# Attention recast per pair of chunks, k gated from PSUM, MLP units of one PSUM bank, and a new instruction planner, in a one-core attention and mixer kernel

## The chip, the cores and the metric

The kernel runs on one core of one Trainium2 chip. The metric is device time in microseconds (us); lower is better. A run counts as fast or slow by its time against the fastest of the same kernel; comparisons here use fast runs, and where a trace fell on a slow run the text says so. "Before" is the unchanged kernel, "after" the changed one. Engines: PE is TensorE (matmul), PEld its weight loads, DVE is VectorE, ACT is ScalarE, POOL is GpSimd, SP is SyncE. SBUF is the on-chip memory that holds tiles and weights; PSUM is the one that the matmuls write, eight banks here, and an *eviction* is a copy out of it.

## The reference

A gated linear recurrence per head, then a token mixer and a channel mixer. Batch 4, 8 heads, sequence 768, head size 48, model size 384, token hidden 256, channel hidden 1536.

```python
f = 1.0 / (1.0 + np.exp(-f_logit))
for t in range(S):
    state = f[:, :, t, :, None] * state + einsum('bhd,bhe->bhde', k[:, :, t], v[:, :, t])
    y[:, :, t] = einsum('bhd,bhde->bhe', q[:, :, t], state)
x = y.transpose(0, 2, 1, 3).reshape(B, S, H * D)
h  = relu(x.T @ w_tok1) @ w_tok2          # over tokens
u  = x + h.T
out = u + relu(u @ w_ch1) @ w_ch2         # over channels
```

The sequence is cut into 6 chunks of 128 rows. The kernel loads two chunks at a time (a *pair*, d = 0 to 2), so there are 12 pairs in all. Within a pair each SBUF partition holds two neighbouring tokens (j = 0 and 1). q is scaled by a decay G, k by its inverse Gi, so that a masked product of the two gives the recurrence inside a chunk; a state of 48 by 48 per head carries it between chunks.

## The kernel before

A planner in Python simulates five engines, decides the order of instructions on each, and chooses buffers. The engines then work through those orders strictly, waiting on semaphores. PSUM is four tiles of two banks each, shared by everything:

```python
P.pool("PP", [pt([128, 2, 512], FP32, f"pp{i}") for i in range(4)])
```

v is needed in chunk order, so two casts put it in place and two more shift half of it over partitions, for each pair. Gi is a bf16 tile in SBUF, and both gates multiply two SBUF operands on VectorE:

```python
nc.gpsimd.tensor_copy(o[0:64, 0:2], x[0:64])        # v, POOL
nc.gpsimd.tensor_copy(o[64:128, 1:3], x[64:128])
cast(e, o[64:128, 0], x[0:64, 1])                   # v shifted, POOL (or ACT in batch 0)
cast(e, o[0:64, 2], x[64:128, 0])
...
nc.scalar.activation(P[f"Gi{i}"], sv(), AF.Exp, bias=0.0, scale=1.0)
...
for j in range(2):                                  # the gates, L408
    nc.vector.tensor_tensor(gated(z, nm, j), x[:, j], gg[:, j], ALU.mult)
```

The second token weight is loaded as it lies and reordered by two copies, which the planner gives to POOL:

```python
P.op("w2", {"DVE": (0.6, 0.1), "POOL": (1.6, 0.1)}, ["w2s0", "w2s1"], ["w2"], lambda e: [cast(
    e, w_tok2[:, kt].rearrange("r c (two p) -> r c p two", two=2),
    P[f"w2s{kt}"].rearrange("r (c p two) -> r c p two", p=64, two=2)) for kt in range(2)], 50)
```

The channel mixer works on whole two-bank tiles, both halves of the tokens together, and its ReLU eviction takes 768 columns. Priorities are fixed numbers per batch:

```python
p_tok, p_ch1, p_ch2 = 100 * b + 60, 100 * b + 165, 100 * b + 178
...
for kt in range(3):
    nc.tensor.matmul(pm[:, th, 0:384]..., lhsT=w_ch1[:, kt, cc * 128:(cc + 1) * 128],
                     rhs=uT[:, 3 * th:3 * th + 3, kt, :], start=(kt == 0), stop=(kt == 2))
```

Lines to know in the profile of before: L604 and L635 are the first and second channel matmuls, L537 and L557 the token matmuls, L408 the gates, L467 the masks, L305 a cast helper.

Of the kernel before, what the change touches and what calls it, by code (L numbers as in the profile page):

```python
# [29 lines left out]
class Op:  # L30
    __slots__ = ("name", "eng", "ins", "outs", "fn", "prio", "after", "done", "start", "groups", "xfer",
                 "pipe")


class Planner:


    def __init__(self):
        self.ops, self.by_name = [], {}
        self.pools, self.group_pool, self.group_of = {}, {}, {}  # L40
        self.producers, self.touch = {}, {}

    def pool(self, name, slots):
        self.pools[name] = [[s, 0.0] for s in slots]

# [5 lines left out]
    def op(self, name, eng, ins, outs, fn, prio, after=(), xfer=None):  # L51
        o = Op()
        o.name, o.eng, o.ins, o.outs, o.fn, o.prio = name, eng, tuple(ins), tuple(outs), fn, prio
        o.after, o.done, o.start, o.xfer = tuple(after), None, None, xfer
        assert name not in self.by_name, name
        self.by_name[name] = o
        self.ops.append(o)

    def run(self):
# [26 lines left out]
        slot_of, last = {}, {}  # L86
        order = []
        while ready:
            best = None
            for o in ready:  # L90
# [7 lines left out]
                for p, n in need.items():  # L98
                    f = sorted(s[1] for s in self.pools[p] if s[1] is not None)
                    if len(f) < n:  # L100
                        ok = False
                        break
                    t = max(t, f[n - 1])
                if not ok:
                    continue
                for e, (occ, lat) in o.eng.items():
                    st = max(t, free.get(e, 0.0))
                    key = (round(st, 3), o.prio, st + occ)
                    if best is None or key < best[0]:
                        best = (key, o, e, st)  # L110
# [3 lines left out]
            free[e] = st + occ  # L114
            end = st + occ + lat
# [10 lines left out]
            for g in o.groups:  # L126
                p = self.group_pool.get(g)
                if p is not None and g not in slot_of:
# [6 lines left out]
                if self.touch[g] == 0 and g in slot_of:  # L135
                    slot_of[g][1] = last[g] + SEM
# [10 lines left out]
        self.slots = {g: s[0] for g, s in slot_of.items()}  # L147
# [3 lines left out]
    def __getitem__(self, v):  # L151
        return self.slots[self.group_of[v]]
# [3 lines left out]
def kernel(  # L156
# [38 lines left out]
    msk = st([128, 128], BF16, "msk")  # L195
# [4 lines left out]
    w_tok2 = st([128, 2, NCH, 128], BF16, "w_tok2")  # L200
# [9 lines left out]
    P.pool("U", [st([128, 3, DM], BF16, f"v_bf{i}") for i in range(3)])  # L210
    P.pool("G", [st([128, 2, H, D], BF16, f"G{i}") for i in range(2)])
    P.pool("Gi", [st([128, 2, H, D], BF16, f"Gi{i}") for i in range(2)])
# [4 lines left out]
    P.pool("gl", [st([128, HP, 2], FP32, f"glast{i}") for i in range(3)])  # L217
    st_tiles = [st([128, HP, D], FP32, f"state{i}") for i in range(2)]
    P.pool("st", st_tiles)
    bd_tiles = [st([128, HP, D], BF16, f"state_bf{i}") for i in range(3)]  # L220
# [6 lines left out]
    P.pool("z", [st([128, S], BF16, f"zT{i}") for i in range(13)])  # L227
    P.pool("PP", [pt([128, 2, 512], FP32, f"pp{i}") for i in range(4)])


    def consts():
# [13 lines left out]
        nc.vector.tensor_copy(msk, tri)  # L245
        nc.vector.tensor_copy(msk[0:64, 64:128], tri[0:64, 0:64])
        nc.vector.tensor_copy(msk[64:128, 0:64], strict[64:128, 64:128])
        for t in st_tiles:
# [13 lines left out]
    for b in range(B):  # L262
        seq = [(nm, c + 1 if nm == "f" else c) for c in range(-1, NP) for nm in "fqkv"]
        prev = None
        for n, (nm, d) in enumerate([s for s in seq if 0 <= s[1] < NP]):
            load(nm, b, d, (100 * b - 150 if b else -1000) + n,
# [17 lines left out]
    for kt in range(2):  # L284
        P.value(f"w2s{kt}", f"w2s{kt}", "z")
    P.op("w2l", {"POOL": (1.2, 0)}, [], ["w2s0", "w2s1"], lambda: [nc.gpsimd.dma_start(
        out=P[f"w2s{kt}"], in_=moe_w_tok2[128 * kt:128 * kt + 128]) for kt in range(2)], -898, ["~w1"],
        xfer=w_mb["w2"] / 0.38)
    P.op("w2", {"DVE": (0.6, 0.1), "POOL": (1.6, 0.1)}, ["w2s0", "w2s1"], ["w2"], lambda e: [cast(
        e, w_tok2[:, kt].rearrange("r c (two p) -> r c p two", two=2),  # L290
        P[f"w2s{kt}"].rearrange("r (c p two) -> r c p two", p=64, two=2)) for kt in range(2)], 50)
    for nm, dst, src, pr, dep in (("wc1", w_ch1, moe_w_ch1, -897, "w2l"),
# [21 lines left out]
    def attention(b, d):  # L314
        i, pr = f"{b},{d}", 100 * b + 20 * d - 70
# [3 lines left out]
        for nm, pl in (("U", "U"), ("G", "G"), ("Gi", "Gi"), ("qkT", "qkT"), ("qkT", "qkT"), ("gl", "gl"), ("xb", "xb"), ("S", "PP"),  # L319
                       ("y", "PP"), ("dS", "PP"), ("x", "x"), ("Pf", "Pf"), ("L", "L")):  # L320
            P.value(f"{nm}{i}", f"{nm}{i}", pl)
        for e in range(2):
            P.value(f"qkT{i},{e}", f"qkT{i}", "qkT")
        P.value(f"qh{i}", f"qk{i}", "qk")
# [4 lines left out]
        P.value(f"S1{i}", f"S{i}", "PP")  # L329
# [3 lines left out]
        def kblk(r, j, hp):  # L333
            t = P[f"kh{i}"][r, H * 128:]
            n = (2 * hp + j) if xbar else (4 * j + hp)
            return t[:, n * 128:(n + 1) * 128]

        def gated(z, nm, j):
            t = P[f"{nm}h{i}"][:, z * H * 128:(z + 1) * H * 128]
            if xbar:  # L340
                return t.rearrange("t (a j r d) -> t j a r d", j=2, r=2, d=64)[:, j, :, :, 0:D]
            return t.rearrange("t (j a r d) -> t j a r d", j=2, r=2, d=64)[:, j, :, :, 0:D]

        def qkT(z, hp, e, rows=slice(0, 128)):
            t = P[f"qkT{i}"]
            n = (8 * e + 4 * z + hp) if xbar else (8 * z + 2 * hp + e)
            return t[rows, n * 128:(n + 1) * 128]
        P.op(f"exp{i}", {"ACT": act_t(768)}, [f"f{i}"], [f"E{i}"],
             lambda: nc.scalar.activation(f_(), f_(), AF.Exp, bias=0.0, scale=-1.0), pr - 25)
        P.op(f"ln{i}", {"ACT": act_t(768)}, [f"E{i}"], [f"Ln{i}"],  # L350
             lambda: nc.scalar.activation(f_(), f_(), AF.Ln, bias=1.0, scale=1.0), pr - 25)  # L351
        flex = {"POOL": pool_t(384, True), "DVE": dve_t(384)} if b == 0 else {"POOL": pool_t(384, True)}
        P.op(f"P{i}", {"DVE": dve_t(384)}, [f"Ln{i}"], [f"Pf{i}"], lambda: nc.vector.tensor_tensor(  # L353
            P[f"Pf{i}"], f_()[:, :, 0], f_()[:, :, 1], ALU.add), pr - 25)
        P.op(f"hi{i}", {"POOL": pool_t(384), "ACT": act_t(384)}, [f"Pf{i}"], [f"hi{i}"],
             lambda e: cast(e, P[f"L{i}"][0][:, :, 0:D], P[f"Pf{i}"]), pr - 25)
        P.op(f"lo{i}", flex, [f"hi{i}", f"Pf{i}"], [f"L{i}"],
             lambda e: (nc.vector if e == "DVE" else nc.gpsimd).tensor_tensor(
                 P[f"L{i}"][1][:, :, 0:D], P[f"Pf{i}"], P[f"L{i}"][0][:, :, 0:D], ALU.subtract), pr - 25)

        def cums():
# [11 lines left out]
        P.op(f"cums{i}", {"PE": (0.53, PE_LAT)}, [f"L{i}", f"hi{i}"], [f"S1{i}"], cums, pr - 20,  # L373
             after=[] if g2 < 0 else [f"~av{b2},1", f"~ds{b2}"])
        P.op(f"S0{i}", {"DVE": dve_t(384)}, [f"S1{i}", f"Ln{i}"], [f"S{i}"], lambda: nc.vector.tensor_tensor(  # L375
            hd(P[f"S{i}"][:, 0, 0:DM]), hd(P[f"S{i}"][:, 1, 0:DM]), f_()[:, :, 1], ALU.subtract), pr)

        def sv():
            return P[f"S{i}"][:, :, 0:DM].rearrange("t j (h d) -> t j h d", d=D)
        P.op(f"G{i}", {"ACT": act_t(768)}, [f"S{i}", f"S1{i}"], [f"G{i}"], lambda: nc.scalar.activation(  # L380
            P[f"G{i}"], sv(), AF.Exp, bias=0.0, scale=-1.0), pr)
        P.op(f"Gi{i}", {"ACT": act_t(768)}, [f"S{i}", f"S1{i}"], [f"Gi{i}"], lambda: nc.scalar.activation(  # L382
            P[f"Gi{i}"], sv(), AF.Exp, bias=0.0, scale=1.0), pr + 0.1)
        P.op(f"gl{i}", {"ACT": (0.06, 0.12)}, [f"S1{i}"], [f"gl{i}"], lambda: nc.scalar.activation(
            P[f"gl{i}"].rearrange("p a e -> p (a e)"), P[f"S1{i}"][:, 1, DM:DM + 2 * HP], AF.Exp, bias=0.0,
            scale=-1.0), pr + 0.2)

        def vcast():
            x = P[f"v{i}"].rearrange("t h j d -> t j h d")
            o = P[f"U{i}"].rearrange("t j (h d) -> t j h d", d=D)  # L390
            nc.gpsimd.tensor_copy(o[0:64, 0:2], x[0:64])
            nc.gpsimd.tensor_copy(o[64:128, 1:3], x[64:128])

        def vshift(e):
            x = P[f"v{i}"].rearrange("t h j d -> t j h d")
            o = P[f"U{i}"].rearrange("t j (h d) -> t j h d", d=D)
            cast(e, o[64:128, 0], x[0:64, 1])
            cast(e, o[0:64, 2], x[64:128, 0])
        P.value(f"V{i}", f"U{i}", "U")
        P.op(f"U{i}", {"POOL": (1.7, 0.1)}, [f"v{i}"], [f"U{i}"], vcast, pr + 1)  # L400
        P.op(f"V{i}", {"POOL": (1.02, 0.1), "ACT": (0.74, 0.12)} if b == 0 else {"POOL": (1.02, 0.1)}, [f"v{i}"],
             [f"V{i}"], vshift, pr + 1.5)
        for z, nm, g in ((0, "q", "G"), (1, "k", "Gi")):
            def gate(z=z, nm=nm, g=g):
                x = P[f"{nm}{i}"].rearrange("t (a r) j d -> t j a r d", r=2)
                gg = P[f"{g}{i}"].rearrange("t j (a r) d -> t j a r d", r=2)
                for j in range(2):
                    nc.vector.tensor_tensor(gated(z, nm, j), x[:, j], gg[:, j], ALU.mult)  # L408
            P.op(f"{nm}h{i}", {"DVE": (2 * dve_t(384)[0], 0.09)}, [f"{nm}{i}", f"{g}{i}"], [f"{nm}h{i}"], gate, pr)

        if not xbar:
            for z, nm in ((0, "qh"), (1, "kh")):
# [304 lines left out]
```

## Time and profile before

| before | |
|---|---|
| median of the timed runs | 210.7 us (209.9 to 212.3) |
| profiled span | 209.3 us |
| first channel matmul starts | 58.6 us |
| last matmul starts | 203.3 us |

From the page of before: busy time, then busy tenths in 40 slices of the span (9 means 90% or more; PEclk is the clock granted to PE), and the chain of work that ended last.

```profile
PE 168.3 (80%) x1852; PEld 103.4 (49%) x1852; DVE 128.6 (61%) x188; ACT 104.5 (50%) x147; POOL 80.5 (38%) x117
...
PE   0365774657589899859579899999999999999990
...
DVE  3579897427996999899975959985232403100121
...
PEclk9999999999969999999959999999999999999996
...
PE 54%; DVE 27%; ACT 8%; issue 6%; DMA 2%; POOL 1%; DVEq 0%; POOLq 0%; ACTq 0%
PE pp L635 20%; PE pp L604 18%; DVE qkh L408 11%; DVE AmT L467 5%; PE pp L537 3%; PE pp L557 3%; ACT G L380 2%; DVE Pf L353 2%; DVE state L507 2%; DMA f_ld<-in_f_logit_dram 2%; PE pp L478 2%; PE pp L464 2%; PE pp L418 1%; PE pp L444 1%; DVE xu L563 1%
```

PE stays at 9 (with an 8 or two) only from about slice 22 on, 115 us. The table by windows of before says the same in numbers. Each row is a window of time: its length, the busy time of PE, PEld, DVE, ACT and POOL in it with the count of instructions, then granted clock, mean DMA share and GB/s.

```profile
0.00:30.00 30.00, 15.13 (x212) 9.60 (x214) 22.32 (x46) 18.90 (x28) 15.91 (x30) 1.00 1.15 227
30.00:58.65 28.65, 16.98 (x228) 10.81 (x228) 18.78 (x23) 16.81 (x24) 15.29 (x18) 1.00 1.00 201
58.65:145.00 86.35, 77.58 (x1025) 47.60 (x1024) 73.74 (x107) 47.05 (x68) 46.77 (x67) 0.94 0.88 169
145.00:203.60 58.60, 58.60 (x392) 35.35 (x391) 12.85 (x14) 21.70 (x27) 2.48 (x3) 1.00 0.29 64
```

There are three parts: a head in which PE is half idle, a mixed part in which VectorE is 85% busy, and a tail of pure MLP matmuls at 100% PE.

The gates, from the view of line L408 of before (minimum, median and maximum duration in ns), and the timelines of POOL and VectorE near 29 us (start, duration, what):

```profile
L408 DVE TENSOR_TENSOR qkh<-q_ld,G x24: 543/716/1181, 10.3 to 135.5; 128x384 bf16<-128x384 f32 x24
L408 DVE TENSOR_TENSOR qkh<-k_ld,Gi x24: 543/773/3515, 11.9 to 137.9; 128x384 bf16<-128x384 f32 x24
```
```profile
27.64 7.05 POOL L305 COPY w_tok<-zT 128x768 bf16<-128x768 bf16 x2
```
```profile
29.65 4.83 DVE L408 TENSOR_TENSOR qkh<-k_ld,Gi 128x384 bf16<-128x384 f32 x2
34.40 0.35 DVE L507 TENSOR_TENSOR state<-state,glast 128x192 f32<-128x192 f32 x1
```

A k gate that takes 0.54 us by itself took 3.5 us once: it started 0.1 us after POOL's second copy and ended 0.2 us before that copy did. The Trainium skill, "SBUF — State Buffer", section "Who interferes with whom", states the cause: a VectorE instruction with two SBUF inputs contends with a GpSimd instruction that reads SBUF, and the shared port pair is an exclusive lock. The trace agrees.

### The profile page before, as it was taken

Reading aid. Unit: us, or ns where it says so; the run is one execution under the profiler, and the core shown is the slowest. Engines: PE = TensorE matmul, PEld = TensorE weight load, DVE = VectorE, ACT = ScalarE, POOL = GpSimd, SP = SyncE. Lnnn points to the kernel's source line nnn. Section 1 sums busy time; section 2 is a strip of 40 time slices with the busy share of each in tenths; the row PEclk is TensorE's granted clock in tenths of the full one; section 3 lists DMA queues with packets and bytes.
Section 4 is the critical chain, followed back from the end, with each engine's and each line's share of the span. In section 5 each row is a group of like instructions: output and inputs, shape, how many; then the busy total and the mean of one; then the engine's idle time right before and its main releaser. Section 6 shows DMA issues by size and latency. Waiting matters only on the chain.

```text
span 209.3 us, 4507 instructions
## 1 busy us (share of the span) xinstructions
PE 168.3 (80%) x1852; PEld 103.4 (49%) x1852; DVE 128.6 (61%) x188; ACT 104.5 (50%) x147; POOL 80.5 (38%) x117
## 2 busy tenths in 40 slices
PE   0365774657589899859579899999999999999990
PEld 0144453424456666435445456555656666566650
DVE  3579897427996999899975959985232403100121
ACT  3787622186849797642280656730144830387000
POOL 3048878067319459787562643510110100000000
PEclk9999999999969999999959999999999999999996
DMA  6999997979976999699998890796250613420143
GB/s 164 261 261 250 209 233 164 276 143 136 244 156 152 261 261 249 117 170 198 245 275 131 212 103 3 114 127 112 60 133 0 89 27 75 99 56 0 27 124 75
DMA packets 73908, 31.35 MB, mean 150 GB/s; under 512 B 67872, under 2 KB 73504, under 8 KB 73888
## 3 DMA queue, kind: packets, MB, share of 16 engines
q1 hardware_dynamic: 70848, 27.93, 65.3%
q0 software_dynamic: 3040, 3.15, 9.3%
q8 instruction: 14, 0.23, 0.5%
q14 instruction: 6, 0.05, 0.1%
HBM read 25.17 MB, written 4.72 MB: 143 GB/s over the span
## 4 chain that ended last, share of the span: by engine, by line
PE 54%; DVE 27%; ACT 8%; issue 6%; DMA 2%; POOL 1%; DVEq 0%; POOLq 0%; ACTq 0%
PE pp L635 20%; PE pp L604 18%; DVE qkh L408 11%; DVE AmT L467 5%; PE pp L537 3%; PE pp L557 3%; ACT G L380 2%; DVE Pf L353 2%; DVE state L507 2%; DMA f_ld<-in_f_logit_dram 2%; PE pp L478 2%; PE pp L464 2%; PE pp L418 1%; PE pp L444 1%; DVE xu L563 1%
## 5 line engine op out<-in xcount | busy, mean ns | idle before, releaser
L604 PE MATMUL pp<-uT,w_ch 128*128 128x384 bf16 x288 | 51.7, 330 | 1.6 <-ACT Gi L382 0.8
L635 PE MATMUL pp<-w_ch,zT 128*128 128x384 bf16 x288 | 51.6, 333 | 0.4 <-DVE xu L563 0.4
L615 ACT ACTIVATE zT<-pp 128x768 bf16<-128x768 f32 x39 | 31.5, 812 | 27.9 <-DVE xu L647 17.3
L647 DVE TENSOR_TENSOR xu<-xu,pp 128x768 f32<-128x768 f32 x12 | 11.4, 952 | 43.1 <-PE pp L635 43.1
L635 PEld LDWEIGHTS <-zT 128*128 128x128 bf16 x288 | 27.8, 100 | 19.0 <-issue 2.1
L604 PEld LDWEIGHTS <-w_ch 128*128 128x128 bf16 x288 | 27.3, 98 | 19.0 <-issue 2.2
L467 DVE TENSOR_TENSOR AmT<-pp,msk 128x1024 bf16<-128x1024 f32 x24 | 28.9, 1216 | 2.5 <-PE pp L464 2.2
L408 DVE TENSOR_TENSOR qkh<-k_ld,Gi 128x384 bf16<-128x384 f32 x24 | 21.3, 926 | 0.0
L517 ACT COPY xu<-pp 128x768 f32<-128x768 f32 x12 | 9.5, 795 | 21.8 <-PE pp L485 12.6
L305 POOL CAST x_bf<-xu 128x768 bf16<-128x768 f32 x11 | 9.1, 827 | 25.6 <-ACT xu L517 25.5
L408 DVE TENSOR_TENSOR qkh<-q_ld,G 128x384 bf16<-128x384 f32 x24 | 17.3, 759 | 1.9 <-ACT G L380 1.8
L514 POOL CAST state_bf<-state 128x192 bf16<-128x192 f32 x20 | 7.8, 388 | 27.1 <-DVE state L507 27.0
L478 PE MATMUL pp<-v_bf,AmT 128*128 128x48 bf16 x192 | 9.9, 194 | 6.8 <-DVE AmT L467 6.7
L563 DVE TENSOR_TENSOR xu<-xu,pp 128x768 f32<-128x768 f32 x12 | 11.0, 949 | 5.3 <-PE pp L557 5.3
L418 PE MATMUL pp<-ident,qkh 128*128 128x128 bf16 x96 | 10.5, 264 | 4.4 <-DVE qkh L408 3.8
L478 PEld LDWEIGHTS <-AmT 128*128 128x128 bf16 x192 | 8.2, 103 | 10.8 <-DVE AmT L467 9.1
L380 ACT ACTIVATE G<-pp 128x768 bf16<-128x768 f32 x12 | 9.8, 813 | 6.9 <-DVE pp L375 6.9
L303 ACT CAST qkT<-pp 128x1024 bf16<-128x1024 f32 x10 | 10.1, 1010 | 5.5 <-PE pp L418 5.5
L353 DVE TENSOR_TENSOR Pf<-f_ld 128x384 f32<-128x384 f32 x12 | 7.5, 629 | 8.4 <-ACT f_ld L351 8.4
L537 PE MATMUL pp<-x_bf,w_tok 128*128 128x384 bf16 x48 | 11.0, 374 | 1.9 <-POOL x_bf L305 1.8
L444 PE MATMUL pp<-v_bf,qkh 64*64 64x48 bf16 x384 | 6.4, 199 | 7.0 <-DVE qkh L408 4.9
L305 POOL CAST v_bf<-v_ld 64x384 bf16<-64x384 f32 x20 | 11.6, 579 | 1.0
(72 smaller groups left out, 234.4 us busy)
## 6 DMA issues: line engine op xcount, KB each, us to landing
f_ld<-in_f_logit_dram SPq DMA_DIRECT2D x12, 384.0 KB, 5.9
q_ld<-in_q_dram SPq DMA_DIRECT2D x12, 384.0 KB, 6.2
k_ld<-in_k_dram SPq DMA_DIRECT2D x12, 384.0 KB, 5.6
v_ld<-in_v_dram SPq DMA_DIRECT2D x12, 384.0 KB, 6.1
out_dram<-xu SPq DMA_DIRECT2D x24, 192.0 KB, 2.8
w_ch<-in_moe_w_ch_dram POOLq DMA_DIRECT2D x2, 1152.0 KB, 11.1
w_tok<-in_moe_w_tok_dram POOLq DMA_DIRECT2D x2, 192.0 KB, 5.8
zT<-in_moe_w_tok_dram POOLq DMA_DIRECT2D x2, 192.0 KB, 6.6
```

Of the source, the lines that this page charges most:

```text
L305: (nc.vector if e == "DVE" else nc.gpsimd).tensor_copy(o, x)
L353: P.op(f"P{i}", {"DVE": dve_t(384)}, [f"Ln{i}"], [f"Pf{i}"], lambda: nc.vector.tensor_tensor(P[f"Pf{i}"], f_()[:, :, 0], f_()[:, :, 1], AL ...
L380: P.op(f"G{i}", {"ACT": act_t(768)}, [f"S{i}", f"S1{i}"], [f"G{i}"], lambda: nc.scalar.activation(P[f"G{i}"], sv(), AF.Exp, bias=0.0, scal ...
L408: nc.vector.tensor_tensor(gated(z, nm, j), x[:, j], gg[:, j], ALU.mult)
L418: nc.tensor.matmul(P[f"T{z}{i}"][:, n // 4, (n % 4) * 128:(n % 4 + 1) * 128], lhsT=P[f"{nm}{i}"][:, m * 128:(m + 1) * 128], rhs=ident, sta ...
L467: P.op(f"mk{ic}", {"DVE": dve_t(1024)}, [f"A{ic}"], [f"Am{ic}"], lambda ic=ic: nc.vector.tensor_tensor(P[f"Am{ic}"], P[f"A{ic}"].rearrange ...
L478: nc.tensor.matmul(yv(h), lhsT=P[f"Am{ic}"][:, (h % 2) * 4 + h // 2, :], rhs=vb[:, h], start=(e == 0 and h < 2), stop=(c == 0), skip_group ...
L537: nc.tensor.matmul(pm[:, rt, 0:DM], lhsT=w_tok1[:, kt, rt * 128:(rt + 1) * 128], rhs=P[f"xb{b},{kt // 2}"][:, kt % 2], start=(kt == 0), st ...
L563: nc.vector.tensor_tensor(x, x, P[f"up{i}"][:, :, 0:DM], ALU.add)
L604: nc.tensor.matmul(pm[:, th, 0:384].rearrange("p (a t) -> p a t", t=128), lhsT=w_ch1[:, kt, cc * 128:(cc + 1) * 128], rhs=uT[:, 3 * th:3 * ...
L615: nc.scalar.activation(o, x, AF.Relu)
L635: nc.tensor.matmul(pm[:, s, 0:DM], lhsT=P[f"z{b},{cc}"][:, tt * 128:(tt + 1) * 128], rhs=w_ch2[:, cc, :], start=(cc == 0), stop=(cc == NCC ...
```

## The change

The intent: cut VectorE and POOL work and their blocking, free PSUM faster, and order the work so that PE is never starved.

1. *Pair-middle coordinates.* Decays are taken relative to the middle of a pair. v stays in its loaded layout (one cast). The state is updated once per pair, with two end-state products instead of one; scores and value products run in 64-row tiles.
2. *k gated from PSUM.* Gi is written over the cumulative sums in PSUM, so the k gate has one SBUF operand. q's gate may go to POOL.
3. *Single-bank units.* MLP tiles hold one bank; the channel mixer does one half of the tokens after the other, in evictions of 384 columns.
4. *w_tok2 loaded straight*, read with stride 2 as two 64-column halves.
5. *Planner.* Priorities become due times (a period of 36 us per batch), banks have a quota per side, and POOL and two-input VectorE work share a modelled port.

Smaller parts: another order of batch 0's loads, the last pair of batch 0 copied out in halves, and the last store split in two.

Cut to its core:

```diff
-    P.pool("Gi", [st([128, 2, H, D], BF16, f"Gi{i}") for i in range(2)])
-    P.pool("z", [st([128, S], BF16, f"zT{i}") for i in range(13)])
-    P.pool("PP", [pt([128, 2, 512], FP32, f"pp{i}") for i in range(4)])
+    P.pool("z", [st([128, S // 2], BF16, f"zT{i}") for i in range(26)])
+    P.psum_tile = pt([128, 8, 512], FP32, "pp")
+    P.psum(8, {"A2": (2, "a"), "A1": (1, "a"), "PP": (2, "m"), "P1": (1, "m")},
+           lambda cls, t: 8 if t < T0 or t > T0 + 3 * LEN else (QA if cls == "a" else QM))
+    T0, LEN, LEAD, AHEAD, PE_FIRST, QA, QM = 31.0, 36.0, 12.0, 16.0, 20.0, 6, 4
...
-                    key = (round(st, 3), o.prio, st + occ)
+                    if e in o.port:
+                        st = max(st, free.get("port", 0.0))
+                    key = (round(st, 2), o.prio, st + occ)
...
-        P.op(f"Gi{i}", ..., lambda: nc.scalar.activation(
-            P[f"Gi{i}"], sv(), AF.Exp, bias=0.0, scale=1.0), pr + 0.1)
+        P.op(f"Gi{i}", ..., lambda: nc.scalar.activation(
+            sv(), sv(), AF.Exp, bias=0.0, scale=1.0), pg - 1, after=[f"G{i}", f"gl{i}"])
...
-        def vcast(): ...      # two casts
-        def vshift(e): ...    # two shifted casts
+        P.op(f"U{i}", {"POOL": pool_t(768), "ACT": act_t(768)} if b == 0 else {"POOL": pool_t(768)}, ...)
...
-        nc.tensor.matmul(pm[:, s, 0:DM], lhsT=w_tok2[:, kt, tt, :], ...)
+        for j in range(2):
+            nc.tensor.matmul(pm[64 * j:64 * j + 64, 0:DM], lhsT=w[:, kt, j], ...)
...
-    p_tok, p_ch1, p_ch2 = 100 * b + 60, 100 * b + 165, 100 * b + 178
+    due(b, what, *n)          # a time for each operation
```

In the changed kernel L698 and L723 are the channel matmuls, L633 and L651 the token matmuls, L485 the gates, L571 the masks, L377 and L379 the cast helpers.

## The prediction

> **What bounds it now.** Timed median 210.7 us, profiled span 209.3. The table by windows splits it in three. From 0 to 58.7 us, before the first channel matmul, PE is busy 32 us; VectorE (41 us) and the DMA engines (share above 1) are the full ones. From 58.7 to 145 us attention of batches 1 to 3 mixes with MLP matmuls: PE busy 78 of 86 us, VectorE 74. From 145 to 203.6 us PE is 100% busy with MLP matmuls alone. The chain of waits: PE 54%, VectorE 27%, the gates (L408) alone 11%.
>
> PE demand from start-to-start times: 672 matmuls of 384 columns at 162 ns are 109 us, their transposes 2, attention about 46 (3.5 to 4 per pair with pauses of about 95 ns into and 120 ns out of small-tile mode): 157. Of this 138 falls after 58.7 us, so PE is already about 95% used there; two half-clock records (3.4 and 6.8 us) explain most of the rest. The gain must come chiefly from the first 58.7 us.
>
> **Removed.** POOL: two w_tok copies (3.7 us each) and v's shifted copies (3.0 us per pair down to about 0.85): 80 us falls to about 55. A gate multiply with no POOL operation beside it takes 546 ns, one overlapping POOL 855 (medians); one k gate pair took 4.8 us at 29.7 us, across the w_tok copies. The Trainium skill, "SBUF — State Buffer", "Who interferes with whom", states this (two SBUF inputs contend with GpSimd's reads); the trace agrees. With Gi in PSUM the 24 k gates should take 0.55 us flat: 21.3 to 13 us. Seven pairs' q gates go to POOL. State updates on VectorE fall from 36 to 12. VectorE in total: 129 to about 115 us.
>
> **Added.** 96 ReLU evictions of 384 columns for 48 of 768 (about 0.51 against 0.81 us: ACT from 104 to about 120). 320 more matmuls: scores and value products in 64-row tiles, inter-chunk products at 96 columns, twice the end-state products: an estimated 0.3 us more PE per pair, 3 us. Mode changes stay ("TensorEngine Tiling (Array Packing)", "Key Properties": switching drains). The column-tiled second token product should cost the same if its halves overlap, as the 64x64 products do in this trace (9 ns each).
>
> **Moved.** Batch 0's attention is 20 us of uncontended VectorE work; I expect it done near 29 us (41 before), then short single-bank stages: first channel matmul near 38 us instead of 58.7. Attention of batch 1 that filled PE's gaps before it now comes after it (+3 us).
>
> **Sum.** Start 38 + (138+3+3)/0.97 = 148 of nearly dense PE, giving 186 to 187; tail 5 (last add 0.55 instead of 0.95, half-size store). Profile 191 to 192; timed **192 us, range 184 to 201**. Chances: faster by over 2% 0.94, within 2% 0.05, slower 0.01. Loads that shrink off PE's path should be worth little by themselves.
>
> **Right if:** first channel matmul at 35 to 41 us; k gates near 550 ns without outliers; PE digits of 9 from there on with hardly a half-clock record; pure-MLP tail near 46 us instead of 58; chain over 70% PE.
>
> **Wrong if:** batch 0's attention still waits (DMA, queues out of step with the planner); PE's small tiles cost much more than 0.3 us per pair (row tiles not overlapping); column-tiled token products serialise (+8 us); two-bank attention tiles starve under the bank quota, leaving PE gaps in 40 to 145 us; or, on the good side, small tiles run cheaper than now, and it falls to 185.

## More of the kernel before

(The tables and PEclk count the clock as full before the first clock record, 49.1 us here. The matmuls say otherwise, as the next fence shows.) I call the time from the first channel matmul to the last matmul of the kernel the *stretch*: 144.6 us. From the timeline of before:

```profile
45.54 2.72 PE L557 MATMUL pp<-h1T,w_tok 128*128 128x384 bf16 x8 [0.90 <-ACT h1T L542]
...
48.95 0.86 PE L557 MATMUL pp<-h1T,w_tok 128*128 128x384 bf16 x4
```

Eight matmuls of 384 columns took 2.72 us, four of the same 0.86: from start to start 320 ns before 49.1 us and 162 after it. Every back-to-back pair before 49.1 us in this trace shows 271 to 320 ns, so PE ran at half rate in the head, as far back as this can be read (25 us).

## The result, and the profile after

Four runs of the changed kernel gave a median of 195.66 us (194.7 to 196.7) against 211.49 us; the ratio is 0.928 (95% interval 0.921 to 0.935). Ratios are the mean time of one kernel's fast runs over that of the other's of the same rounds, so not quite the ratio of the medians quoted. A control, the same file on another chip, gave 0.926. The forecast was 192 us with a range of 184 to 201.

The same parts of the page, after:

```profile
PE 171.3 (88%) x2172; PEld 106.0 (55%) x2172; DVE 109.7 (56%) x201; ACT 114.4 (59%) x210; POOL 57.4 (30%) x96
...
PE   0389677688999999999999899899999999999990
...
DVE  5588623369999688779694556694153044112021
...
PEclk9999996559999999999999999999999999999999
...
PE 69%; DMA 11%; ACT 5%; DVE 4%; SPq 4%; issue 2%; POOL 2%; DVEq 0%; ACTq 0%; POOLq 0%
PE pp L723 24%; PE pp L698 21%; PE pp L651 6%; DMA v_ld<-in_v_dram 6%; PE pp L633 4%; SPq L338 4%; DMA k_ld<-in_k_dram 3%; PE pp L581 3%; PE pp L564 3%; PE pp L593 3%; DMA qkT<-qkh 2%; PE pp L519 2%; PE pp L496 1%; DVE AmT L571 1%; ACT f_ld L427 1%
```

The table by windows of after, cut at its own stages:

```profile
0.00:30.00 30.00, 18.28 (x306) 12.89 (x307) 18.55 (x48) 20.29 (x31) 11.11 (x28) 1.00 1.14 226
30.00:46.40 16.40, 11.98 (x139) 7.73 (x137) 8.99 (x16) 9.21 (x18) 4.33 (x7) 0.58 1.05 240
46.40:145.00 98.60, 96.11 (x1447) 59.29 (x1447) 71.82 (x119) 64.75 (x123) 41.35 (x62) 1.00 0.90 180
145.00:189.60 44.60, 44.60 (x285) 26.09 (x282) 9.76 (x19) 20.17 (x40) 0.57 (x1) 1.00 0.27 58
```

PE is now full from 46.4 us on (97% busy up to 145 us, then all), and VectorE is down to 73% of the mixed part. Gates left the chain; loads of k and v entered it, which suggests that the head is now held in part by DMA. The view of line L485 shows the gates as forecast:

```profile
L485 DVE TENSOR_TENSOR qkh<-k_ld,pp x24: 536/547/556, 11.6 to 131.7; 128x384 bf16<-128x384 f32 x24
...
L485 POOL TENSOR_TENSOR qkh<-q_ld,G x14: 900/910/914, 26.8 to 126.1; 128x384 bf16<-128x384 f32 x14
L485 DVE TENSOR_TENSOR qkh<-q_ld,G x10: 545/553/840, 10.2 to 100.1; 128x384 bf16<-128x384 f32 x10
```

The spread of the k gates (543 to 3515 ns) is gone: 536 to 556 ns, whether POOL works or not.

Where the 14.9 us between the two profiled spans came from, read from the starts of the matmuls:

| part | before | after | difference |
|---|---|---|---|
| start of the first channel matmul | 58.6 | 46.4 | -12.2 |
| stretch to the last matmul | 144.6 | 143.2 | -1.4 |
| last matmul to the end | 6.0 | 4.8 | -1.2 |

The small change of the stretch hides two larger ones. Within it I summed the times from each matmul's start to the next one's, each cut at 400 ns so that long waits count apart:

| in the stretch, us | before | after |
|---|---|---|
| channel matmuls (576) | 98.0 | 97.8 |
| attention matmuls | 26.3 | 29.4 |
| token matmuls and transposes of u | 14.2 | 14.4 |
| waits beyond 400 ns | 6.2 | 1.6 |

After has more attention work in the stretch, because batch 1's first pair no longer fits before it and because a pair costs slightly more; it lost 4.6 us of waits in return.

The clock differs too. In before, the clock record shows half clock for 10.2 us of the stretch (59.3 to 62.7 and 103.7 to 110.5 us), in after for none. In those windows 17 channel matmuls took 5.3 us, 312 ns each, against 166 ns for the other 558 of before; so about 2.5 us of before's 98.0 is the clock (an estimate from these counts). At equal clock the channel matmuls of after are the slower ones by about 2 us. One cause can be seen: in the ten places where a full-size matmul stands before a half-width token product it takes 253 to 257 ns to the next start in place of 162, about 0.9 us in all.

Last, the head of after. These timeline lines run from v's third load to the first channel matmul:

```profile
26.05 0.82 POOL L379 CAST v_bf<-v_ld 128x768 bf16<-128x768 f32 x1 [3.40 <-DMA v_ld<-in_v_dram]
26.84 1.77 POOL L485 TENSOR_TENSOR qkh<-q_ld,G 128x384 bf16<-128x384 f32 x2
...
31.49 1.07 PE L564 MATMUL pp<-qkT 48*64 48x128 bf16 x32
...
32.26 2.35 DVE L571 TENSOR_TENSOR AmT<-pp,msk 128x1024 bf16<-128x1024 f32 x2 [6.50 <-PE pp L564]
...
39.57 4.05 PE L651 MATMUL pp<-h1T,w_tok 128*64 128x384 bf16 x24 [1.37 <-ACT h1T L638]
...
46.44 2.11 PE L698 MATMUL pp<-uT,w_ch 128*128 128x384 bf16 x12 [0.56 <-ACT uT L377]
```

VectorE idles 6.5 us before the third pair's masks, which started at 32.3 us, when I had expected the pair's attention to be over at 29. The trace's clock record shows half clock from 30.4 to 44.0 us, so that 24 token matmuls took 4.05 us. It begins only at 27.0 us, and before that the matmuls of 384 columns that ran back to back took 273 to 321 ns from start to start: as in before, PE was at half rate in most of the head, not only from 30.4 us (the 1.00 of the table's first row comes from missing records).

### The profile page after: what moved, and what is told of

The parts are those of the page before. It is cut to its first block, busy times and chain, and to the rows that moved or that the text cites. A ratio compares the mean times of both kernels' runs of the same rounds, so it can differ in the third digit from the quotient of the medians.

```text
span 194.4 us, 5235 instructions
## 1 busy us (share of the span) xinstructions
PE 171.3 (88%) x2172; PEld 106.0 (55%) x2172; DVE 109.7 (56%) x201; ACT 114.4 (59%) x210; POOL 57.4 (30%) x96
## 4 chain that ended last, share of the span: by engine, by line
PE 69%; DMA 11%; ACT 5%; DVE 4%; SPq 4%; issue 2%; POOL 2%; DVEq 0%; ACTq 0%; POOLq 0%
PE pp L723 24%; PE pp L698 21%; PE pp L651 6%; DMA v_ld<-in_v_dram 6%; PE pp L633 4%; SPq L338 4%; DMA k_ld<-in_k_dram 3%; PE pp L581 3%; PE pp L564 3%; PE pp L593 3%; DMA qkT<-qkh 2%; PE pp L519 2%; PE pp L496 1%; DVE AmT L571 1%; ACT f_ld L427 1%
## 5 line engine op out<-in xcount | busy, mean ns | idle before, releaser
L698 PE MATMUL pp<-uT,w_ch 128*128 128x384 bf16 x288 | 53.1, 326 | 1.7 <-DVE zT L707 0.6
L723 PE MATMUL pp<-w_ch,zT 128*128 128x384 bf16 x288 | 51.6, 327 | 0.0
L705 ACT ACTIVATE zT<-pp 128x384 bf16<-128x384 f32 x74 | 35.4, 492 | 26.0 <-PE pp L698 25.6
L698 PEld LDWEIGHTS <-w_ch 128*128 128x128 bf16 x288 | 27.1, 98 | 20.0 <-issue 3.1
L571 DVE TENSOR_TENSOR AmT<-pp,msk 128x1024 bf16<-128x1024 f32 x24 | 28.6, 1218 | 14.3 <-PE pp L564 14.2
L723 PEld LDWEIGHTS <-zT 128*128 128x128 bf16 x288 | 26.4, 98 | 18.0 <-issue 1.5
L733 DVE TENSOR_TENSOR xu<-xu,pp 128x384 f32<-128x384 f32 x24 | 13.2, 551 | 35.3 <-PE pp L723 35.3
L617 ACT COPY xu<-pp 128x768 f32<-128x768 f32 x11 | 8.8, 797 | 14.9 <-PE pp L581 14.9
L379 POOL CAST x_bf<-xu 128x768 bf16<-128x768 f32 x10 | 8.2, 824 | 30.3 <-ACT xu L617 30.2
L707 DVE TENSOR_SCALAR zT<-pp 128x384 bf16<-128x384 f32 x22 | 11.5, 553 | 8.9 <-ACT h1T L638 6.3
L657 DVE TENSOR_TENSOR xu<-xu,pp 128x384 f32<-128x384 f32 x24 | 12.4, 550 | 6.4 <-PE pp L651 6.2
L633 PE MATMUL pp<-x_bf,w_tok 128*128 128x384 bf16 x48 | 12.8, 371 | 2.9 <-DMA w_tok<-in_moe_w_tok_dram 1.6
L651 PE MATMUL pp<-h1T,w_tok 128*64 128x384 bf16 x96 | 12.0, 382 | 1.4 <-ACT h1T L638 1.4
L485 POOL TENSOR_TENSOR qkh<-q_ld,G 128x384 bf16<-128x384 f32 x14 | 12.5, 910 | 1.7 <-ACT G L465 0.7
L485 DVE TENSOR_TENSOR qkh<-k_ld,pp 128x384 bf16<-128x384 f32 x24 | 12.2, 548 | 1.1 <-ACT pp L467 0.9
L427 ACT ACTIVATE f_ld<-f_ld 128x768 f32<-128x768 f32 x12 | 10.1, 839 | 3.5 <-DMA f_ld<-in_f_logit_dram 3.5
L379 POOL CAST v_bf<-v_ld 128x768 bf16<-128x768 f32 x11 | 9.4, 853 | 7.7 <-DMA v_ld<-in_v_dram 7.6
L564 PE MATMUL pp<-qkT 48*64 48x128 bf16 x384 | 10.3, 243 | 1.3 <-DMA qkT<-qkh 0.8
L377 ACT CAST u_bf<-xu 128x768 bf16<-128x768 f32 x9 | 7.5, 833 | 5.9 <-DVE xu L657 5.7
## 6 DMA issues: line engine op xcount, KB each, us to landing
w_ch<-in_moe_w_ch_dram POOLq DMA_DIRECT2D x2, 1152.0 KB, 12.2
```

Source lines behind the costliest of these rows:

```text
L379: (nc.vector if e == "DVE" else nc.gpsimd).tensor_copy(o, x)
L485: vec(e).tensor_tensor(o[:, j], x[:, j], g[:, j], ALU.mult)
L564: nc.tensor.matmul(A[64 * e:64 * e + 64, par, hp * 128:(hp + 1) * 128].rearrange("p (j t) -> p j t", j=2), lhsT=qkT(1, e)[rows, hp, j], rh ...
L571: lambda j=j: nc.vector.tensor_tensor(P[f"Am{j}{i}"], P[f"A{j}{i}"].rearrange("p b (a t) -> p (b a) t", t=128), msk[:, j].rearrange("p j t ...
L633: nc.tensor.matmul(P[f"{g},0"][:, 0:DM], lhsT=w_tok1[:, kt, rt * 128:(rt + 1) * 128], rhs=P[f"xb{b},{kt // 2}"][:, kt % 2], start=(kt == 0 ...
L651: nc.tensor.matmul(pm[64 * j:64 * j + 64, 0:DM], lhsT=w[:, kt, j], rhs=P[f"h1{b}"][:, kt, :], start=(kt == 0), stop=(kt == 1))
```

## The experiments

Theories. **A**: the gain is the earlier start, bought by taking POOL work and blocking out of the head. **B**: it is single-bank units (and the planner), which keep PE fed in the stretch. **C**: it is relief of VectorE. **D**, formed after the result: the start is later than forecast because v lands late and passes this on through POOL's queue. Twelve kernels ran; all were correct. "Start" is that of the first channel matmul in the profiled run.

| run | part altered | ratio to before | start | stretch |
|---|---|---|---|---|
| control | none (the change) | 0.926 | 45.3 | 143.3 |
| e1_stage_w2 | after, w_tok2 staged again | 0.916 | 45.3 | 140.5 |
| e2_before_direct_w2 | before, w_tok2 straight | 0.975 | 54.2 | 142.6 |
| e3_gi_sbuf | after, Gi in SBUF | 0.925 | 48.0 | 139.4 |
| e5_two_bank | after, two banks per MLP unit | 0.967 | 47.8 | 151.6 |
| e11_two_bank_nq | the same, no quota | 0.952 | 45.0 | 149.3 |
| e12_noquota | after, no quota | 0.910 | 44.6 | 140.5 |
| e4_old_prio | after, old priorities, no quota | 0.939 | 47.6 | 143.8 |
| e6_q_dve | after, batch 0's q gates on VectorE | 0.924 | 44.0 | 143.6 |
| e7_warm | after, needless matmuls in the head | 0.939 | 51.5 | 143.7 |
| e13_gate_v | after, weights held back | 0.956 | 44.6 | 156.3 |
| e16_combined | e1 + e12 + e6 | 0.938 | 46.9 | 146.4 |

The traces of e5, e7 and e13 were taken in runs counted as slow (1.5% or more above the fastest of the same kernel).

### The straight load of w_tok2 alone, put into the kernel before

```diff
-    P.op("w2", {"DVE": ..., "POOL": ...}, ...)      # two reordering copies
+    weight("w2", [(w_tok2, moe_w_tok2.rearrange("(kt r) c -> r kt c", r=128))], -898, ["~w1"])
...
-    nc.tensor.matmul(pm[:, s, 0:DM], lhsT=w_tok2[:, kt, tt, :], ...)
+    for j in range(2):
+        nc.tensor.matmul(pm[64 * j:64 * j + 64, s, 0:DM], lhsT=w[:, kt, j], ...)
```

> The kernel before with only this part of the change: w_tok2 loaded straight, no POOL copies, half-width token product. Theory A: the k gate pair of 4.8 us at 29.7 us falls to 1.1 to 1.5, the first channel matmul comes 3 to 5 us earlier (54 to 56 us), time 3 to 4 us lower, ratio about 0.983. Theory B: the start is held by two-bank PSUM tiles and order, so it moves under 1.5 us and the ratio is over 0.993.

Measured: median 206.02 us, ratio 0.975 (0.969 to 0.981); start 54.2 us, 4.5 us earlier. The k gates that had been blocked, in this run's VectorE timeline:

```profile
29.18 1.02 DVE L401 TENSOR_TENSOR qkh<-k_ld,Gi 128x384 bf16<-128x384 f32 x2
```

The pair fell from 4.83 to 1.02 us and the start moved by about as much. Theory A holds for this part: in the kernel before, two POOL copies on the port shared with VectorE cost about 4 us of head. The profiled stretch was 2.0 us shorter as well, with 3.4 us at half clock in place of 10.2; that part was not aimed at.

### The same copies put back into the changed kernel

```diff
+    P.op("w2", {"POOL": (1.6, 0.1)}, ["w2s0", "w2s1"], ["w2"], ...)   # two copies again
-    for j in range(2):
-        nc.tensor.matmul(pm[64 * j:64 * j + 64, 0:DM], lhsT=w[:, kt, j], ...)
+    nc.tensor.matmul(pm[:, 0:DM], lhsT=w_tok2[:, kt, tt, :], ...)
```

> The changed kernel with w_tok2 staged and copied on POOL again (two copies of 3.7 us), the second token product back to full-width tiles. Theory A (the gain is an earlier start of the channel matmuls, 58.6 to 46.4 us, bought chiefly by taking POOL work and port blocking out of the first 50 us): POOL's queue is held about 7 us in the first 35 us, the first channel matmul comes 3 to 7 us later (49 to 53 us), the time rises by 3 to 5 us, ratio to before about 0.945. Theory B (the gain is in PSUM units and the planner, which keep PE fed after the start): first channel matmul unchanged within 1.5 us, time within 1 us of the changed kernel, ratio 0.925 to 0.932. The token product itself should cost about 0.9 us less, since in the traces 72 half-width ones took 7.21 us against 6.29.

Measured: median 193.36 us, ratio 0.916 (0.910 to 0.921), no loss at all. POOL's timeline shows that the copies do run:

```profile
24.94 1.88 POOL L493 TENSOR_TENSOR qkh<-q_ld,G 128x384 bf16<-128x384 f32 x2
26.77 7.07 POOL L387 COPY w_tok<-w2s 128x768 bf16<-128x768 bf16 x2
```

In those 7 us VectorE had no instruction with two SBUF inputs: its third k gate reads PSUM and was done at 24.9 us, a short state update ended at 25.2, and its next work was the masks at 31.1 us, which read PSUM. Expectation A missed: what costs time is the meeting of the copies with a two-input multiply, not the copies. The new half-width product cost 1.0 us in the stretch (7.21 us for 72 matmuls in the control, 6.17 for 36 full-width ones here), as expected.

The halves themselves overlap: inside a run of them in the trace of after, two take 161 to 165 ns from start to start of the next two, as long as one full-width matmul (162). What costs is the change of tile size, which the last half (256 to 259 ns to the next start) and the full-size matmul ahead of the first half (253 to 257 ns) pay. The second of these is booked under the channel matmuls, so the half-width form costs about 1.9 us in the stretch (estimate: 1.0 and ten times 93 ns), and this run's gain is near that.

### k gated from SBUF again

```diff
+    P.pool("Gi", [st([128, 2, H, D], BF16, f"Gi{i}") for i in range(2)])
-            sv(), sv(), AF.Exp, bias=0.0, scale=1.0)
+            P[f"Gi{i}"]..., sv(), AF.Exp, bias=0.0, scale=1.0)
```

> The changed kernel with the k gate reading its factor from SBUF again (bf16 tile), planner told that it uses the shared port. Theory A as in the forecast (VectorE is no longer near PE's path once PE is dense): k gates scatter again from 0.55 to over 1 us, VectorE busy rises by 3 to 8 us, time rises by 0 to 2 us, ratio 0.928 to 0.938. Rival C (relief of VectorE is a main source of the gain): time rises by 4 us or more, ratio at least 0.947.

Measured: median 195.53 us, ratio 0.925 (0.919 to 0.930), equal to the control. From the groups of this run:

```profile
L485 DVE TENSOR_TENSOR qkh<-k_ld,Gi 128x384 bf16<-128x384 f32 x24 | 17.6, 778 | 1.6 <-ACT Gi L467 1.6
```

The k gates went back to a mean of 778 ns, 5.4 us more VectorE time than the 12.2 us of the change, and the kernel was no slower. The planner had answered by giving two more pairs' q gates to POOL, so VectorE's total rose by only 1.0 us (110.7), not by the 3 to 8 expected. So in this run the part of the change that looks best by itself brought nothing net, once the planner had somewhere else to put the load. The start came 2.7 us later than in the control and the stretch was 3.9 us shorter, so a small loss may be hidden by the new order. The run speaks against rival C, but a larger load on VectorE was not tried.

### Two banks per MLP unit, with and without the quota

```diff
-    P.psum(8, {..., "P1": (1, "m")}, lambda cls, t: 8 if ... else (QA if cls == "a" else QM))
+    P.psum(8, {..., "P1": (2, "m")}, ...)                    # e5: two banks held, one used
+    P.psum(8, {..., "P1": (2, "m")}, lambda cls, t: 8)       # e11: the same, no quota
+    P.psum(8, {..., "P1": (1, "m")}, lambda cls, t: 8)       # e12: one bank, no quota
```

> The changed kernel with every mixing unit holding two PSUM banks, of which it uses one (quotas unchanged). Theory A: start of channel matmuls within 2 us of 46.4, the stretch from there to the last matmul grows from 143 by 1 to 3 us, ratio 0.933 to 0.945. Theory B: the stretch grows by 6 us or more, since in the kernel before the pauses over 0.4 us alone added 6.2 us there, ratio at least 0.955.

> Two banks held per mixing unit, as in the earlier run, but all eight banks free to both sides (no quota), to take the quota of four banks out of that run's result. If holding two banks is itself the cost: the stretch stays at 148 us or more, ratio at least 0.95. If the earlier loss came from a quota that left only two units: stretch 140 to 145, ratio 0.92 to 0.94.

> The changed kernel without the bank quota: the control of the run above. Expected to move little: stretch within 3 us of 139 to 143, ratio 0.92 to 0.94; if the quota matters, a ratio of at least 0.95.

Measured: 204.88 us (ratio 0.967), 201.51 us (0.952) and 192.35 us (0.910). Holding two banks lengthened the stretch from 140.5 to 149.3 us without the quota, and from 143.3 to 151.6 with it. The tables by windows, e11 with two banks first, then e12 with one:

```profile
45.00:80.00 35.00, 29.90 (x548) 20.18 (x548) 27.92 (x45) 28.12 (x52) 20.60 (x31) 1.00 1.06 225
80.00:120.00 40.00, 38.16 (x578) 22.91 (x576) 27.31 (x45) 24.54 (x46) 16.45 (x24) 1.00 0.95 180
```
```profile
44.60:80.00 35.40, 35.18 (x584) 23.31 (x584) 31.03 (x52) 29.53 (x58) 17.28 (x27) 1.00 1.08 233
80.00:120.00 40.00, 39.49 (x591) 24.22 (x589) 28.88 (x50) 23.80 (x47) 18.29 (x27) 1.00 0.93 188
```

The matmuls are the same 2172; with two banks held PE is idle for 5.1 us between 45 and 80 us, where it was idle 0.2 us. By the waits view of e11 its waits over the whole stretch are mostly for evictions, each a little. The largest (total us, times, longest us):

```profile
PE pp L581 <- DVE AmT L571: 2.3, 4, 0.8
PE pp L698 <- DVE xu L733: 1.3, 1, 1.3
```

This supports B for the stretch: without single-bank units the rest of the change gains about half of what it gained (ratio 0.952 and 0.967 in place of 0.910 and 0.926). The same sign came in two different orders, but each run was planned anew, and a new order alone made one stretch 5.9 us longer (e16 against e12, below); so the direction is well supported and the size of 8 to 9 us is not settled. Single-bank units bought little of the start: 47.8 and 45.0 us with two banks, 45.3 and 44.6 with one. The quota did no good (0.910 without it).

### The old priorities

```diff
-    due(b, what, *n): a time per operation
+    due(b, what, *n): 100*b + 60 ... 100*b + 178 as before;  at(b, d): 100*b + 20*d - 70
+    lambda cls, t: 8                                          # no quota
```

> The changed kernel's data layout, tiles and units, but the planner with the priorities of the kernel before (fixed numbers per batch in place of due times) and no bank quota. If the due times are what keeps PE fed (planner theory): pauses return, the stretch from the first channel matmul to the last one grows from 140 to 143 us by 5 us or more, ratio at least 0.95. If single-bank units alone keep it fed: stretch within 3 us, ratio 0.92 to 0.94. A later end of attention (over 150 us) with a longer pure tail would go with the first.

Measured: median 198.66 us, ratio 0.939 (0.934 to 0.944); start 47.6, stretch 143.8 us. Against its proper control (e12, 0.910) that is 6 us slower, half in the start and half in the stretch; the largest single wait of PE in the stretch is 2.5 us, for a cast of v. The profiled run was also at half clock for 6.8 us of its stretch (54.6 to 61.5 us, PE busy throughout), where e12 had none; that alone can account for up to 3.4 us. This falls between the two expectations, and by the last run below it is within what a mere reshuffle can do. The worth of the due times stays open.

### What holds the start

```diff
-  ("q", {"DVE": ..., "POOL": ...}, True)
+  ("q", {"DVE": ...} if b == 0 else {"DVE": ..., "POOL": ...}, True)      # e6
...
-  P.op("gate_k", ..., ["k0,1"], ...)
+  P.op("gate_k", ..., ["v0,2"], ...)                                      # e13: weights after v's third load
...
+  nc.tensor.matmul(o, lhsT=warm_t[:, 0:128], rhs=warm_t, start=True, stop=True)   # e7: before each
+                                                                          # waiting group of batch 0
```

> The changed kernel itself, unaltered, on the chip of the next two runs: the control for small differences. Expected ratio to before 0.92 to 0.935, first channel matmul 45 to 48 us.

> The changed kernel with batch 0's q gates kept on VectorE, so that the third pair's q gate no longer stands in POOL's queue behind the cast of v, whose load landed only at 26 us. Theory D (the late start comes from v's late landing passed on through POOL's in-order queue): scores of the third pair start 3 to 4 us earlier than 31.5, first channel matmul 2 to 4 us earlier, ratio 0.008 to 0.02 below the control. Rival (half clock or the load itself holds the start): within 0.005 of the control.

> The changed kernel with the weight loads held until the third pair's v has landed (instead of the second pair's k), nothing else. Theory D with its cause in the loads: v lands near 20 us instead of 26, third pair's scores 4 us or more earlier; the token weights arrive later (about 27 us instead of 24) and the first channel weights near 37 us, which is then what the first channel matmul waits for, so it comes at 38 to 42 us and the ratio falls 0.015 to 0.03 below the control. If the weights become the new wait and land after 44 us, the ratio is within 0.01 of the control.

> The changed kernel with about 75 needless matmuls of 384 columns put into PE's pauses during batch 0's attention (into banks that the next real matmuls overwrite), to keep the granted clock up. If the late start (46.4 us against the 38 forecast) is largely the half clock up to 44 us: no half-clock record between 10 and 44 us, the 24 second token matmuls take about 2 us instead of 4.05, first channel matmul 3 to 6 us earlier (40 to 43 us), ratio 0.90 to 0.915. If the start is held by loads and by the order of POOL's queue: under 1.5 us earlier, ratio 0.922 or more.

Measured: control 195.32 us (0.926), e6 194.77 us (0.924), e13 202.24 us (0.956), e7 200.58 us (0.939). None brought the start nearer to 38 us than 44.0.

In e6 the third pair's q gate ran at 24.5 us instead of 26.8, but the scores moved only from 31.5 to 30.9 us. The timeline of e6 shows what took over:

```profile
28.18 0.83 ACT L377 CAST x_bf<-xu 128x768 bf16<-128x768 f32 x1
28.20 0.61 PE L496 MATMUL pp<-ident,qkh 128*128 128x128 bf16 x8 [0.30 <-ACT xu L617]
...
28.92 1.92 ACT L377 CAST qkT<-pp 128x1024 bf16<-128x1024 f32 x2
...
30.89 0.64 PE L564 MATMUL pp<-qkT 48*64 48x128 bf16 x32 [0.97 <-ACT qkT L377]
```

The second pair's copies on ACT stand in front of the third pair's transposes. In e13 v's cast was done by 23.3 us, but the scores still came at 30.9, behind eight token matmuls that took 2.76 us, at half clock; and the stretch was 13 us longer in the run profiled (a slow one; its fast runs are 5 to 7 us better), with weights and later loads that came late, and with 13.7 us at half clock in it where the control had none. With the weights held back, v's third load landed in 6.9 us from its issue instead of 11.0. So theory D as I put it falls. As I read these two traces, three chains of nearly the same length (v and q on POOL, copies on ACT, token matmuls ahead in PE's queue) hold the third pair, and taking one away uncovers the next.

e7 put in 88 needless matmuls and kept the clock at full from 4.4 to 31.7 us and from 35.1 us on. Its ratio rests on two fast runs, and the trace is of a slow one. The token product took 2.14 us instead of 4.05, as expected, and yet the start was 51.5 us. In its POOL timeline v lands later than in the change:

```profile
28.61 0.82 POOL L385 CAST v_bf<-v_ld 128x768 bf16<-128x768 f32 x1 [5.24 <-DMA v_ld<-in_v_dram]
```

That load took 13.5 us from its issue against 11.0, and the needless matmuls stood in front of real ones (1.6 us before one group of transposes). Half clock therefore costs about 2 us in the token product directly, but its removal could not be shown to move the start, since the needless matmuls bring a delay of their own; why v's landing moved is open.

### The three small gains together

> A version meant to beat both: the changed kernel with three parts taken the other way, namely no bank quota, w_tok2 staged on POOL with full-width second token products, and batch 0's q gates on VectorE. If the three small gains measured apart (ratios 0.910, 0.9155 and 0.924 against 0.926 to 0.928 for the change) are of different causes and add up: first channel matmul 43 to 45.5 us, stretch from there to the last matmul 138 to 140.5 us, ratio 0.895 to 0.91. If they are the same few microseconds counted twice (both cut the stretch from 143 to 140.5 us): stretch 140 to 141.5, ratio 0.908 to 0.918.

Measured: median 197.80 us, ratio 0.938 (0.934 to 0.942), slower than the change itself (0.926). Three edits that had measured better by 0.5, 2.2 and 3.3 us apart (ratios times 211 us) should have given 6 us together and lost 2.5: the waits in the stretch rose to 5.0 us, 2.3 of them for transposing DMAs of q and k. (One run of before in these rounds took 532.84 us; it is left out.) Both expectations missed. Each edit makes the planner reorder all engines, so a few us between two variants say little about the part that was edited: e16 has a stretch 5.9 us longer than e12, which differs from it by two edits that had each done no harm. PE's largest waits in the stretch of e16:

```profile
PE pp L572 <- DMA qkT<-qkh: 2.3, 2, 1.4
PE pp L589 <- DVE AmT L579: 2.0, 3, 0.8
```

What stands best are effects with a visible cause: the two-bank one, found in two different orders (8 to 9 us) with PE's idle time beside it, and the w_tok2 copies in the kernel before (4.8 us), with the blocked gate gone in the trace. The best version run is the change without the quota, 192.35 us; it beats both, but by the same argument its 1.7% over the change (0.910 against 0.926) may be luck of the order and not a merit of having no quota.

## Why the prediction was right or wrong

The predicted 192 us and the measured 195.7 us agree to 2%, and the direction and the stage of the gain were right. The sum behind it was "start 38 + 148 + tail 5"; measured were 46.4 + 143.2 + 4.8. Two terms were off in opposite directions, the start by +8.4 us and the stretch by -4.8, so the total is better than its parts: that closeness is luck.

- *The gain must come chiefly from the head.* Right: 12.2 of 14.9 us are the earlier start. Why it is earlier is only partly shown. Removing the w_tok2 copies from the kernel before gave 4.5 us; no run isolates the rest. VectorE did 41.1 us of work before the start in before and 27.5 in after, which fits the forecast's argument, but pair-middle coordinates, the single cast of v and the new order of loads were never undone one at a time.
- *First channel matmul near 38 us.* Mis-sized: it measured 46.4 (45.3 in the control), outside the 35 to 41 given. I took VectorE's work, 20 us, for the length of the head. VectorE was idle for 6.5 us of it; the third pair waited for loads, ACT and POOL in series, and half clock, which I had not counted in the head at all, stretched the token product by about 2 us. What each of these costs the start stays open. My warning "queues out of step" named it without sizing it.
- *148 us of nearly dense PE.* Measured 143.2. Attention in the stretch rose by 3.1 us where I had allowed 6, and waits fell to 1.6 us where dividing by 0.97 allowed 4.5.
- *Small tiles cost 0.3 us more per pair.* Near: by pair, scores 0.71 to 0.73 us, value products 0.63 to 0.61, inter-chunk products 0.53 to 0.59, end-state products 0.54 to 0.72, together 0.24 more.
- *The column-tiled token product should cost the same if its halves overlap.* They do overlap (two in 161 to 165 ns inside a run, one full-width matmul in 162), and still it cost more: 7.2 against 6.3 us in the stretch, and about 0.9 us in the matmuls ahead of it. I had named the mode changes and not added them up.
- *k gates 0.55 us flat; VectorE 115, ACT 120, POOL 55.* Right: 547 ns; 110, 114 and 57. And "loads that shrink off PE's path should be worth little" agrees with the run that put Gi back in SBUF at no cost.
- *Hardly a half-clock record from the start on; tail near 46 us; chain over 70% PE.* None after 44 us up to the end of the matmuls; the last attention matmul starts at 143.6 us and the last of all at 189.6, 46.0 us later; the chain is 69% PE, just short of the 70.
- *What I had not seen* is how much the stretch rests on PSUM. I counted single-bank units as "short stages" of the head only. Undone, the stretch was 8 to 9 us longer in two orders, about half of the whole gain, with the doubt about order said above.

## What to carry to other kernels

Cut the span into stages by what PE does and ask of each part of a change in which stage it can pay: the same removal of POOL copies was worth 4.8 us in the old kernel and nothing in the new one, where nothing met them. Where PE was the limit and the engines around it were at 60 to 75%, halving the PSUM unit went with a larger gain here (8 to 9 us) than any other part tested; how many units PE can run ahead is worth asking early. Check the clock by the matmuls themselves, since its record can begin late. In a kernel whose order comes from a planner, run a few harmless edits first to learn how far order alone moves the time, and don't add up gains smaller than that.

## What the Trainium skill lacked or had wrong

- "TensorEngine Tiling (Array Packing)", "Key Properties", says that changing the tiling mode drains TensorE, without a figure. Here a 384-column matmul ahead of a switch into small tiles took 255 to 259 ns from its start to the next start in place of 162, and from the last small matmul's start to the first full-size one's it took 111 to 149 ns.
- The same page, "Theoretical Speedup", gives up to 2x for two column tiles and no cost of entering and leaving them. Inside a run of 128x64 products of 384 columns the trace of after agrees: two in 161 to 165 ns, where one full-width matmul takes 162. With the way out of the mode the average is 200 ns for two (72 of them in the stretch), against 175 ns for the full-width matmul in before, since the runs are short (4 to 16 products).
- "TensorE: Matmul & The Clock Gate", "Wait — 56ns, not 53.3ns?", says that start-to-start never drops below about 25 ns. That holds for full-size tiles here (25 to 26 ns for 2 columns), not for 64x64 tiles: 32 of them, with 48 columns each, started within 0.25 us at full clock in the trace of before, 8.2 ns apart; the page treats packed tiles in a later part, and the sentence should say that it leaves them out.
- The same page, "What's actually happening", gives an activity window of 3413 ns. The traces agree: half-clock records of 3.4, 6.8, 10.2 and 13.7 us. It calls the ramp a loss under 1% of a typical kernel; here PE was at half rate wherever this can be read before the first channel matmul, up to 49.1 us in before and up to 44.0 in after, but for 3.4 us from 27.0; in after it was busy for 10.0 of the 13.6 us from 30.4 to 44.0. What this costs in time was not shown.
- "SBUF — State Buffer", "Who interferes with whom": confirmed with 4.83 us for a gate pair across two POOL copies and 1.02 us without them.
- No page gives a time for a load that runs beside weight loads from another queue: v's third load took 11.0 us to land where the median v load took 6.3, and 6.9 us when the weights were held back (e13).
